# Attention and two MLPs on one core: h banks and scratch blocks as tensors of their own, the cosine of a pair in two halves, other figures in the build-time planner

## The chip, the cores and the metric

The kernel runs on one core of a Trainium2 chip. The metric is device time in microseconds (us), the median of several runs. Three runs of the kernel before took 893.64, 894.47 and 897.54 us; 894.47 us is the time before.

## The reference, cut to what matters

```python
def reference(q, k, v, w_in, w_out, s, b, w2_in, w2_out):
    x = attention(q, k, v)          # 4 x 8 heads, 576 positions, head size 64; heads 0-3: window of 32,
                                    # heads 4-7: 32 positions at a distance of 4; softmax
    x = x.transpose(0, 2, 1, 3).reshape(2304, 512)
    h = x @ w_in                    # 512 -> 2048
    x = (s * np.maximum(h, 0) ** 2 + b) @ w_out     # 2048 -> 512
    h = x @ w2_in                   # 512 -> 2048
    return (h * np.cos(h)) @ w2_out # 2048 -> 512
```

All of it is fp32. The kernel splits an fp32 operand into a high part in fp32r and the rest, and makes one product of three fp32r matmuls.

## The kernel before, in words

**First part, attention and the first MLP** (line 1060 on). The 2304 tokens go in five tiles of 384, 384, 512, 512 and 512 (`SIZES`). Within a tile the loop runs over 16 chunks of the hidden size: `mm_in` makes h in a PSUM bank, `relu2` squares it, `mm_out` accumulates y in four banks. Attention for the next tile, the unpacking of the weights from 64-bit words (`w_float`, `w_join`) and the preparation of the second MLP's weights (`pair_*`) are laid beside these matmuls. `y_out(t)` (line 651) evicts the four y banks of a tile, two on ACT and two on DVE, and writes the tile to the DRAM tensor `parked`: on SP's queue in one DMA for tiles 0 to 3, and for tile 4 in four DMAs on ACT's queue, one behind each eviction.

**Second part, the second MLP** (`second_mlp`, line 728). The tokens go in three stretches of 768 (s = 0, 1, 2), each in two halves of 384 columns (`TH`). Both matrix products are done by Strassen and Winograd's scheme with seven products where a plain 2 x 2 division has eight. For a pair j of hidden chunks the seven products i = 1, 5, 6, 3, 7, 2, 4 are six matmuls of 384 columns each: such a group of six is called a step below. `h_mm` (line 841) loads the step's weights `w_in` on SP's queue (eight buffers in turn), makes the matmuls into a bank, and evicts it: i = 1, 5, 6 by a copy on ACT (`hp`, `hu`), i = 4 by a copy on ACT into `hh`, i = 3, 7, 2 by an add on DVE into `hh`. Products 6, 7 and 4 of a pair go on accumulating in the bank of product 1, and 3 in that of 5. The order on TensorE is 1(j), 2(j-1), 5(j), 6(j), 4(j-1), 3(j), 7(j), then 1(j+1), where (j) says the pair. The banks are: `j % 2` for 1, 6, 7, 4; number 2 for 5 and 3; number 3 for 2. The eight PSUM banks are four tiles of two banks each, `bank[0..3]`; h has the last two:

```python
        bank = [psum.tile([P, 2, 512], F32, tag=f"b{n}", name=f"bank{n}") for n in range(4)]
            b = j % 2 if i in (1, 6, 7, 4) else 2 if i in (5, 3) else 3
            acc = bank[2 + b // 2][:, b % 2, :TH]
```

So bank 0 of h lies beside bank 1 in one tile, and bank 2 beside bank 3. After 4(j) comes `cosine(s, j)` (line 864): ACT takes h + 0.25 to whole turns, DVE subtracts, ACT takes the sine, and DVE multiplies by h in two halves into `group`. `turns` is one buffer. The second product (`y_mm`, line 795) reads `group` through `ring` (split on ACT and DVE) and the weights `w_out`. The first 58 h steps of stretch 0 run alone; from there h steps of stretch 1 and y steps of stretch 0 alternate, and so on, until y steps of stretch 2 run alone. `x_steps(s)` (line 761) loads the four quarters of a stretch from `parked` into a `group` buffer and makes the seven left operands of it (`xo`) with subtractions and splits on ACT and DVE. For stretch 0 this is done during the first part (`first_x`, lines 1087 to 1101).

**What sets the order.** The program is scheduled by hand: every engine and queue executes its instructions in the order in which they are given out. That order comes from the planner `Recorder` (lines 83 to 273), which runs when the kernel is built. It records the instructions, keeps the order of TensorE's, and gives each of the others a due time from what needs it. `length` (line 187) says how long each instruction occupies its engine and how much later its result is there; `HOP` is added where one engine waits for another. `order` then goes through time: whenever an engine is free it takes, of the instructions whose needs are met within `LOOK` (0.4 us), the one due first. `give_out` issues a batch; a batch is given out whole before the next one is recorded. Tile 4's `y_out` belongs to the batch of line 1102, and the whole second part (its first `w_in` load too) to the next, line 1108. Waits between engines are not the planner's: the framework adds them from the tiles that the instructions, in the order given, write and read. All instructions of planned batches carry line 272 in the profile, so that rows are told apart by tile names.

Of the kernel before, what the change touches and what calls it, by code (L numbers as in the profile page):

```python
# [9 lines left out]
F32 = mybir.dt.float32  # L10
# [4 lines left out]
AF = mybir.ActivationFunctionType  # L15
ALU = mybir.AluOpType
# [5 lines left out]
NT = B * S  # L22
P = 128
# [59 lines left out]
class Recorder:  # L83
# [1 line left out]

    HOP, LOOK, SOON, EARLIER = 0.12, 0.4, 4.0, 4.0
    ENGINES = {"tensor": "PE", "vector": "DVE", "scalar": "ACT", "sync": "SP", "gpsimd": "POOL"}

    def __init__(self, nc):
# [94 lines left out]
    @staticmethod  # L186
    def length(engine, what, out, args, kw, aps):
        cols = math.prod(k for _, k in out.ap[1:])
        if what == "dma_start":
            moved = cols * out.ap[0][1] * mybir.dt.size(out.dtype) / 280.0e3  # L190
            return (0.06, 2.6 + 1.5 * moved) if engine == "scalar" else (moved, 2.6 + 0.5 * moved)
        if engine == "tensor":
            if what == "transpose":
                return 0.00085 * cols, 0.0
            if args[1].dtype == F32R:
                return cols / 2400.0 + 0.0133, 0.0
            return (4 * cols / 2400.0 + 0.0053) * (0.6 if cols <= 64 else 1.0 if cols > 300 else 1.25), 0.0
        if engine == "scalar":
            extra = 0.09 if is_pointer(kw) else 0.0
            return 0.19 + 0.000833 * cols + extra + (0.19 if kw.get("accum_out") is not None else 0.0), 0.0  # L200
        from_psum = any(x.space == bass.MemoryType.PSUM for x in aps)
        if what == "tensor_reduce":
            cols = math.prod(k for _, k in kw["in_"].ap[1:])
            return 0.15 + 0.00107 * cols, 0.0
        two = what in ("tensor_tensor", "scalar_tensor_tensor") or from_psum
        return 0.152 + (0.001047 if two else 0.00054) * cols, 0.0

    def order(self):

        steps, ids = self.steps, self.kept  # L210
        own = set(ids)
        hop = lambda a, b: self.HOP if steps[a][0] != steps[b][0] else 0.0
        due = {}
        for n in reversed(ids):
            if steps[n][0] == "PE" or steps[n][5] or n not in due:
                due[n] = min(due.get(n, 1.0e9), steps[n][4])
            for d in steps[n][3] & own:
                due[d] = min(due.get(d, 1.0e9), due[n] - hop(d, n) - steps[d][1] - steps[d][2])
        left, then, ready = {}, {n: [] for n in ids}, {}
        for n in ids:  # L220
            left[n] = len(steps[n][3] & own)
            ready[n] = max((self.ends[d] + hop(d, n) for d in steps[n][3] - own), default=-1.0e9)
            for d in steps[n][3] & own:
                then[d].append(n)
        pe = [n for n in reversed(ids) if steps[n][0] == "PE"]
        waiting, free = {e: [] for e in self.free}, dict(self.free)
        for n in ids:
            if not left[n] and steps[n][0] != "PE":
                waiting[steps[n][0]].append(n)
        given = []  # L230
        while len(given) < len(ids):
            best = None
            for e, able in waiting.items():
                if e == "PE":
                    able = [n for n in pe[-1:] if not left[n]]
                if not able:
                    continue
                first = max(free[e], min(ready[n] for n in able)) + (0.0 if e == "PE" else self.LOOK)
                n = min((n for n in able if ready[n] <= first), key=lambda n: (due[n], n))
                at = max(free[e], ready[n])  # L240
                if best is None or (at, n) < best[:2]:
                    best = (at, n, e)
            at, n, e = best
            given.append((at, n))
            free[e] = at + steps[n][1]
            self.ends[n] = free[e] + steps[n][2]
            if e == "PE":
                pe.pop()
            else:
                waiting[e].remove(n)  # L250
            for k in then[n]:
                ready[k] = max(ready[k], self.ends[n] + hop(n, k))
# [28 lines left out]
def attention_then_two_mlps(ctx, tc, qk_p, qk_d, v_p, v_d, mask_p, mask_d, w1, w2, sv, bv, out):  # L281
# [39 lines left out]
        nc.scalar.copy(xy_tile(t)[:, :, :n], spill[:, :, :n])  # L321

    scratch = pool("scratch", 1, ctx, space=bass.MemoryType.DRAM)
    parked = scratch.tile([P, NCC, NT], F32, tag="parked", name="parked")
    cut_in = [scratch.tile([P, 7, 2, 256], F32, tag=f"cut_in{j}", name=f"cut_in{j}") for j in range(NPAIR)]
    cut_out = scratch.tile([P, 7, NPAIR, 2, 256], F32, tag="cut_out", name="cut_out")

# [321 lines left out]
            nc.tensor.matmul(y[:, : SIZES[t]], lo, g[:, 0, :], start=False, stop=fc == NFC - 1)  # L649

    def y_out(t):
        to = parked[:, :, STARTS[t] : STARTS[t + 1]]
        for e in range(NCC):
            y = yps[t][e]
            if t == 0:
                nc.vector.tensor_scalar_mul(bsum[:, e : e + 1], y[:, SIZES[0] : SIZES[0] + 1], b_sb)
            dst, bias = xy[t][:, e, :], bsum[:, e : e + 1]
            if e % 2 == 0:
                nc.scalar.activation(out=dst, in_=y[:, : SIZES[t]], func=AF.Identity, scale=s_sb, bias=bias)
            else:  # L660
                nc.vector.tensor_scalar(
                    out=dst, in0=y[:, : SIZES[t]], scalar1=s_sb, scalar2=bias, op0=ALU.mult, op1=ALU.add
                )
            if t == NTILE - 1:
                nc.scalar.dma_start(to[:, e, :], dst)
        if t < NTILE - 1:
            nc.sync.dma_start(to, xy[t])
        del xy[t], yps[t]

    def g_tile(t, fc):  # L670
# [33 lines left out]
    def x_loads(s, places):  # L704
        def load(place, key):
            rows, half = BLOCKS[key]
            t0 = s * TS + half * TH
            nc.sync.dma_start(place, parked[:, 2 * rows : 2 * rows + 2, t0 : t0 + TH])

        return [lambda p=p, key=key: load(p, key) for p, key in zip(places, X_BLOCKS)]  # L710

# [16 lines left out]
    def second_mlp(pool, psum, first_x):  # L728
# [8 lines left out]
        yp1, yp5, yu2, yc21 = (pool.tile([P, 2, TH], F32, tag=x, name=x) for x in ("yp1", "yp5", "yu2", "yc21"))  # L737
        for n in range(6, N_X):
            x_slot[n] = pool.tile([P, 2, 2, TH], F32R, tag=f"xo{n}", name=f"xo{n}")
        bank = [psum.tile([P, 2, 512], F32, tag=f"b{n}", name=f"bank{n}") for n in range(4)]  # L740

        places = {
            0: dict(X=(0, 2), Y=(1, 3)),
# [51 lines left out]
        def y_mm(s, i, j):  # L795
            r, w = splits[s, i, j // 2]
            b, new = Y_BANK[s == NS - 1][i]
            for half in range(2):
                cs = slice(half * P, (half + 1) * P)
                for k, (a, x) in enumerate(((0, 0), (0, 1), (1, 0))):  # L800
                    nc.tensor.matmul(
                        bank[b][:, half, :TH], w[:, j % 2, a, cs], r[:, x, j % 2, :],
                        start=new and j == 0 and k == 0, stop=j == NPAIR - 1 and k == 2, skip_group_check=True,
                    )

        def y_end(s, i):
            last = s == NS - 1
            acc = lambda i: bank[Y_BANK[last][i][0]][:, :, :TH]

            def send(tile, row, half):  # L810
                t0 = s * TS + half * TH
# [5 lines left out]
                nc.scalar.copy(yp5, acc(5))  # L817
            elif i == 6:
                nc.scalar.copy(yu2, acc(6))
                plus(yu2, acc(3), yu2)  # L820
                if last:
                    plus(yu2, yp5, yu2)
                send(yu2, 256, 1)
            elif i == 2:
                plus(yp1, acc(2), yp1)
                send(yp1, 256, 0)
            elif i == 7:
                if last:
# [12 lines left out]
        def h_mm(s, j, i):  # L841
# [1 line left out]
            loads[0] += 1  # L843
            nc.sync.dma_start(w.bitcast(F32), cut_in[j][:, IN_AT[i]])
            b = j % 2 if i in (1, 6, 7, 4) else 2 if i in (5, 3) else 3
            acc = bank[2 + b // 2][:, b % 2, :TH]
            x = x_slot[operand[s, i]]
            for kc in range(2):
                cs = slice(kc * P, (kc + 1) * P)
# [23 lines left out]

        x_makes(0, first_x)[-1]()
        h_list = []
# [7 lines left out]

        def h_step(s, j, i):
            h_mm(s, j, i)
            if i == 4:
                cosine(s, j)
                if j == NPAIR - 1:
                    whole[0] = s + 1
                    if s + 1 < NS:  # L890
                        x_steps(s + 1)
# [305 lines left out]
```

## Time and profile before

| | |
|---|---|
| median of 3 runs | 894.47 us (893.64 to 897.54) |
| the profiled execution | 895.13 us |
| its span, first to last instruction | 893.3 us |
| TensorE (PE) busy | 859.4 us, 96% |
| PE's weight loads (PEld) busy | 755.9 us, 85% |
| VectorE (DVE) busy | 646.6 us, 72% |
| ScalarE (ACT) busy | 529.7 us, 59% |
| mean granted clock of TensorE | 0.991 |

Times in rows are microseconds from the start of the span. A matmul's row starts when it is taken up; matmuls overlap, so the busy time of one (0.34 us) is about twice the distance to the next. The granted clock is a share of 2.4 GHz. "x12" is the number of instructions that a row merges, and a bracket at its end the idle time before it and what ended that. SPq and ACTq are the queues on which DMAs are issued. Buffer numbers are left out of names: `hp` stands for `hp10`, `hp11` and `hp5`, `hu` for `hu2`, `bank` for all four.

### The profile page before, as it was taken

What the parts mean: (1) busy time and instruction counts of PE and PEld (TensorE: products, weight loads), DVE (VectorE), ACT (ScalarE), POOL (GpSimd) and SP (SyncE); (2) the same over time, 40 slices, a digit from 0 to 9 for tenths busy, and PEclk for the clock granted to TensorE, in tenths of its full rate; (3) what the DMA queues carried; (4) which work ended last, traced back from release to release, by engine and by line L of the source; (5) the groups of instructions that cost most, each with busy time, mean ns of one, the idle gap of its engine ahead of it and who ended that gap; (6) DMA issues with size and microseconds to landing.
All of it is one profiled execution on the core that took longest, in us unless ns stands there. A gap on an engine that the chain in (4) does not pass through costs nothing.

```text
span 893.3 us, 13668 instructions
## 1 busy us (share of the span) xinstructions
PE 859.4 (96%) x5004; PEld 755.9 (85%) x5004; DVE 646.6 (72%) x1062; ACT 529.7 (59%) x1060; POOL 3.5 (0%) x10
## 2 busy tenths in 40 slices
PE   8999999999999999999999678899999999999998
PEld 6656689998888888888888577699999999999997
DVE  6899899767655676668778335588777878767783
ACT  6888885666556555556555235576555655655642
POOL 1000000000000000000000000000000000000000
PEclk9999999999999999999999979999999999999999
DMA  9977425456426256653876666668788888896786
GB/s 253 345 252 237 131 92 165 145 172 225 134 100 220 76 197 204 202 188 124 264 263 199 210 214 196 203 205 256 229 265 269 290 268 249 276 277 204 228 261 212
DMA packets 97826, 189.85 MB, mean 213 GB/s; under 512 B 8320, under 2 KB 48736, under 8 KB 97760
## 3 DMA queue, kind: packets, MB, share of 16 engines
q1 hardware_dynamic: 97184, 187.94, 66.3%
q10 hardware_dynamic: 576, 1.05, 0.3%
q8 instruction: 40, 0.66, 0.3%
q14 instruction: 26, 0.21, 0.1%
HBM read 150.16 MB, written 38.80 MB: 212 GB/s over the span
## 4 chain that ended last, share of the span: by engine, by line
PE 90%; DMA 4%; DVE 3%; ACT 2%; issue 0%; SPq 0%; DVEq 0%; ACTq 0%
PE bank L272 40%; PE y L272 22%; PE h L272 22%; PE sc L272 3%; PE pv L272 2%; PE tp L272 1%; DVE hh L272 1%; DMA first_v<-v_d 1%; DMA stage<-w 1%; DVE wa L272 1%; DMA group<-parked 1%; DMA first_v<-v_p 1%; DMA first_qk<-qk_d 0%; DMA first_qk<-qk_p 0%; ACT wa L272 0%
## 5 line engine op out<-in xcount | busy, mean ns | idle before, releaser
L272 PE MATMUL bank<-xo,w_in 128*128 128x384 f32 x1008 | 202.9, 342 | 24.6 <-DVE hh L272 19.5
L272 PEld LDWEIGHTS bank<-xo,w_in 128*128 128x128 f32 x1008 | 177.7, 190 | 34.7 <-DVE hh L272 25.9
L272 PE MATMUL bank<-ring,w_out 128*128 128x384 f32 x1008 | 193.4, 336 | 0.9 <-ACT yc L272 0.9
L272 PEld LDWEIGHTS bank<-ring,w_out 128*128 128x128 f32 x1008 | 176.6, 188 | 2.8 <-ACT yc L272 1.4
L272 PE MATMUL h<-xs,wh 128*128 128x512 f32 (+1 forms) x512 | 153.5, 381 | 0.0
L272 PE MATMUL y<-g,wh 128*128 128x512 f32 (+1 forms) x512 | 152.3, 379 | 0.0
L272 ACT CAST ring<-group 128x768 fp32r<-128x768 f32 x84 | 69.8, 834 | 67.5 <-PE bank L272 66.7
L272 PEld LDWEIGHTS h<-xs,wh 128*128 128x128 f32 x512 | 93.7, 188 | 15.0
L272 PEld LDWEIGHTS y<-g,wh 128*128 128x128 f32 x512 | 94.1, 188 | 14.4
L272 ACT ACTIVATE r<-h 128x512 f32<-128x512 f32 (+1 forms) x80 | 44.2, 553 | 102.5 <-PE h L272 100.1
L272 DVE TENSOR_TENSOR ring<-group,ring 128x768 fp32r<-128x768 f32 x84 | 79.7, 955 | 23.9 <-ACT ring L272 22.8
L272 PE MATMUL h<-xs,wl 128*128 128x512 f32 (+1 forms) x256 | 96.4, 376 | 0.0
L272 PE MATMUL y<-g,wl 128*128 128x512 f32 (+1 forms) x256 | 96.2, 376 | 0.0
L272 ACT ACTIVATE sm<-sm,nmax 96x80 f32<-96x80 f32 (+1 forms) x140 | 49.4, 354 | 13.6 <-DVE nmax L272 13.6
L272 PEld LDWEIGHTS h<-xs,wl 128*128 128x128 f32 x256 | 48.1, 188 | 7.6
L272 PEld LDWEIGHTS y<-g,wl 128*128 128x128 f32 x256 | 48.0, 188 | 7.6
L272 ACT COPY hp<-bank 128x384 f32<-128x384 f32 x48 | 23.0, 480 | 50.8 <-PE bank L272 45.4
L272 DVE CAST g<-r 128x512 fp32r<-128x512 f32 (+1 forms) x64 | 25.9, 405 | 35.5 <-ACT r L272 35.4
L272 DVE TENSOR_TENSOR group<-turns,hh 128x768 f32<-128x768 f32 x48 | 44.1, 953 | 7.9 <-ACT turns L272 7.9
L272 DVE SCALAR_TENSOR_TENSOR turns<-turns,hh 128x1536 f32<-128x1536 int32 x24 | 42.0, 1751 | 7.8 <-ACT turns L272 7.8
L272 PE MATMUL y<-g,wa 128*128 128x385 f32 x128 | 44.2, 488 | 0.0
L272 PE MATMUL h<-xy,wa 128*128 128x384 f32 x128 | 44.0, 490 | 0.0
(109 smaller groups left out, 1111.7 us busy)
## 6 DMA issues: line engine op xcount, KB each, us to landing
w_in<-cut_in SPq DMA_DIRECT2D x168, 256.0 KB, 3.6
w_out<-cut_out SPq DMA_DIRECT2D x84, 512.0 KB, 4.3
stage<-w SPq DMA_DIRECT2D x32, 512.0 KB, 5.2
raw<-w SPq DMA_DIRECT2D x32, 512.0 KB, 5.8
cut_in<-w SPq DMA_DIRECT2D x8, 896.0 KB, 5.4
cut_out<-w SPq DMA_DIRECT2D x8, 896.0 KB, 5.3
qk<-qk_d SPq DMA_DIRECT2D x20, 352.0 KB, 4.3
qk<-qk_p SPq DMA_DIRECT2D x20, 304.0 KB, 3.4
```

Source lines behind the costliest of these rows:

```text
L272: getattr(getattr(self.nc, engine), what)(*args, **kw)
```

## The change

- `parked` becomes six tensors of 384 columns. `y_out` writes a tile in as many DMAs as it meets blocks (tiles 2, 3 and 4: two each), all on SP's queue after the whole tile's evictions; tile 4's four DMAs on ACT's queue go. `x_loads` reads from the block that it needs.
- h has four PSUM tiles of one bank each; y keeps two of two banks. In the last stretch y's products 3 and 2 use h banks; they are evicted by two adds of 384 columns in place of one of 768.
- The cosine is made in halves of 768 columns: the second half of `hh` after step 7 (its chunks come from 3 and 7), the first half after step 4.
- In the planner, `HOP` was 0.12 us for all. It is now 0.21 us behind PE, 2.0 us behind an SP DMA that ACT or DVE waits for, and 0.05 us for all else, an SP DMA that PE waits for among it. 0.09 us of each ACT and DVE instruction's length are counted as delay of its result and no longer as time of its engine.

```diff
-    HOP, LOOK, SOON, EARLIER = 0.12, 0.4, 4.0, 4.0
+    LOOK, SOON, EARLIER = 0.4, 4.0, 4.0
+    HOP = {"PE": 0.21, "SP": 2.0}
...
-            return 0.19 + 0.000833 * cols + extra + (0.19 if kw.get("accum_out") is not None else 0.0), 0.0
+            return 0.10 + 0.000833 * cols + extra, 0.09
...
-        return 0.152 + (0.001047 if two else 0.00054) * cols, 0.0
+        return 0.062 + (0.001047 if two else 0.00054) * cols, 0.09
...
-        hop = lambda a, b: self.HOP if steps[a][0] != steps[b][0] else 0.0
+        hop = lambda a, b: 0.0 if steps[a][0] == steps[b][0] else self.HOP.get(
+            steps[a][0] if steps[b][0] != "PE" or steps[a][0] != "SP" else "", 0.05
+        )
...
-    parked = scratch.tile([P, NCC, NT], F32, tag="parked", name="parked")
+    parked = [scratch.tile([P, NCC, TH], F32, tag=f"parked{b}", name=f"parked{b}") for b in range(NT // TH)]
...
-            if t == NTILE - 1:
-                nc.scalar.dma_start(to[:, e, :], dst)
-        if t < NTILE - 1:
-            nc.sync.dma_start(to, xy[t])
+        for b in range(NT // TH):
+            lo, hi = max(STARTS[t], b * TH), min(STARTS[t + 1], (b + 1) * TH)
+            if lo < hi:
+                nc.sync.dma_start(
+                    parked[b][:, :, lo - b * TH : hi - b * TH], xy[t][:, :, lo - STARTS[t] : hi - STARTS[t]]
+                )
...
-            nc.sync.dma_start(place, parked[:, 2 * rows : 2 * rows + 2, t0 : t0 + TH])
+            nc.sync.dma_start(place, parked[2 * s + half][:, 2 * rows : 2 * rows + 2, :])
...
-        bank = [psum.tile([P, 2, 512], F32, tag=f"b{n}", name=f"bank{n}") for n in range(4)]
+        y_bank = [psum.tile([P, 2, 512], F32, tag=f"by{n}", name=f"y_bank{n}") for n in range(2)]
+        h_bank = [psum.tile([P, 512], F32, tag=f"bh{n}", name=f"h_bank{n}") for n in range(4)]
...
-            acc = bank[2 + b // 2][:, b % 2, :TH]
+            acc = h_bank[b][:, :TH]
...
-        def cosine(s, j):
-            h, rest = hh[(s * NPAIR + j) % 2], turns.bitcast(F32)
-            nc.scalar.activation(out=turns, in_=h, func=AF.Identity, bias=quarter)
-            nc.vector.scalar_tensor_tensor(out=rest, in0=turns, scalar=-1.0, in1=h, op0=ALU.mult, op1=ALU.add)
+        def cosine(s, j, n):
+            half = slice(2 * n, 2 * n + 2)
+            h, turn = hh[(s * NPAIR + j) % 2][:, half, :], turns[:, half, :]
+            rest = turn.bitcast(F32)
+            nc.scalar.activation(out=turn, in_=h, func=AF.Identity, bias=quarter)
+            nc.vector.scalar_tensor_tensor(out=rest, in0=turn, scalar=-1.0, in1=h, op0=ALU.mult, op1=ALU.add)
             nc.scalar.activation(out=rest, in_=rest, func=AF.Sin, scale=TWO_PI, bias=right_angle)
-            for n, key in enumerate(("11", "12")):
-                g, _, k = g_place(s, key, j)
-                half = slice(2 * n, 2 * n + 2)
-                nc.vector.tensor_tensor(out=g[:, :, k, :], in0=rest[:, half, :], in1=h[:, half, :], op=ALU.mult)
+            g, _, k = g_place(s, ("11", "12")[n], j)
+            nc.vector.tensor_tensor(out=g[:, :, k, :], in0=rest, in1=h, op=ALU.mult)
...
-            if i == 4:
-                cosine(s, j)
+            if i in (7, 4):
+                cosine(s, j, int(i == 7))
```

## Rows read from the trace of the kernel before

**Rows 1.** Stages: length; PE, PEld, DVE, ACT, POOL busy; granted clock; DMA.
```profile
25.00:125.00 100.00, 98.71 (x480) 63.18 (x478) 92.48 (x186) 85.69 (x201) 0.00 (x0) 1.00 0.66 217
125.00:500.00 375.00, 375.00 (x2299) 324.60 (x2299) 264.30 (x515) 219.40 (x538) 0.00 (x0) 1.00 0.53 174
...
509.30:523.00 13.70, 7.24 (x21) 6.44 (x21) 5.05 (x7) 1.21 (x3) 0.00 (x0) 0.50 0.85 309
523.00:592.60 69.60, 57.84 (x300) 51.11 (x300) 41.37 (x48) 39.63 (x50) 0.00 (x0) 1.00 0.67 191
...
592.60:893.30 300.70, 292.04 (x1664) 287.99 (x1662) 225.84 (x256) 165.03 (x200) 0.00 (x0) 1.00 0.81 252
```

**Rows 2.** PE's waits, 500 to 592.6: total us, times, longest.
```profile
PE bank L272 <- DVE hh L272: 16.3, 13, 8.5
PE bank L272 <- ACT hu L272: 2.9, 5, 0.6
PE bank L272 <- ACT hh L272: 1.7, 3, 0.6
```

**Rows 3.** Timeline, 561 to 566: start, us, what, idle before.
```profile
561.69 0.48 ACT L272 COPY hu<-bank 128x384 f32<-128x384 f32 x1 [0.75 <-PE bank L272]
...
562.22 2.35 PE L272 MATMUL bank<-xo,w_in 128*128 128x384 f32 x12 [0.57 <-ACT hu L272]
...
564.61 0.48 ACT L272 COPY hh<-bank 128x384 f32<-128x384 f32 x1 [0.96 <-PE bank L272]
...
565.14 2.39 PE L272 MATMUL bank<-xo,w_in 128*128 128x384 f32 x12 [0.57 <-ACT hh L272]
```

**Rows 4.** Timeline of PE where the second part begins.
```profile
499.89 4.41 PE L272 MATMUL bank<-xo,w_in 128*128 128x384 f32 x24
504.65 1.99 PE L272 MATMUL bank<-xo,w_in 128*128 128x384 f32 x10 [0.35 <-DMA w_in<-cut_in]
515.11 3.25 PE L272 MATMUL bank<-xo,w_in 128*128 128x384 f32 x9 [8.47 <-DVE hh L272]
```

**Rows 5.** Timeline of DVE in the same stretch.
```profile
500.10 0.81 DVE L272 TENSOR_SCALAR xy<-y,s_sb,bsum 128x512 f32<-128x512 f32 x1 [0.55 <-PE y L272]
511.43 0.96 DVE L272 TENSOR_TENSOR group<-group 128x768 f32<-128x768 f32 x1 [10.53 <-DMA group<-parked]
...
514.51 0.55 DVE L272 TENSOR_TENSOR hh<-bank,hp 128x384 f32<-128x384 f32 x1
```

**Rows 6.** Timeline of SP's queue in the same stretch.
```profile
478.79 25.81 SPq L272 DMA_DIRECT2D w_in<-cut_in  x8
504.69 1.41 SPq L272 DMA_DIRECT2D group<-parked  x3
```

**Rows 7.** Waits of SP's queue, 478 to 506.
```profile
SPq L272 <- DMA parked<-xy: 18.9, 4, 16.6
```

**Rows 8.** Groups by shape, 500.0 to 592.6: busy us, mean ns, idle before.
```profile
L272 DVE SCALAR_TENSOR_TENSOR turns<-turns,hh 128x1536 f32<-128x1536 int32 x7 | 12.3, 1751 | 0.7 <-ACT turns L272 0.7
L272 ACT ACTIVATE turns<-hh,quarter 128x1536 int32<-128x1536 f32 x7 | 11.1, 1580 | 3.1 <-DVE group L272 3.0
L272 DVE TENSOR_TENSOR group<-turns,hh 128x768 f32<-128x768 f32 x12 | 11.0, 955 | 5.4 <-ACT turns L272 5.4
...
L272 ACT CAST xo<-group 128x768 fp32r<-128x768 f32 x6 | 5.0, 834 | 5.0 <-DMA group<-parked 5.0
...
L272 ACT COPY hu<-bank 128x384 f32<-128x384 f32 x8 | 3.8, 476 | 5.1 <-PE bank L272 5.0
```

**Rows 9.** DMAs, 490:600 and 318:327: count, KB, us to landing.
```profile
w_in<-cut_in SPq DMA_DIRECT2D x66, 256.0 KB, 3.1
...
parked<-xy SPq DMA_DIRECT2D x1, 1024.0 KB, 4.4
```

**Rows 10.** Chain that ended last: the y steps that run alone.
```profile
830.36 58.56 PE bank L272 x336
```

**Rows 11.** Waits of PE, 592.6 to the end.
```profile
PE bank L272 <- DVE hh L272: 3.3, 5, 0.7
```

More of the change, by code (lines that the diff above doesn't have):

```diff
@@ L198, in length @@
         if engine == "scalar":
-            extra = 0.09 if is_pointer(kw) else 0.0
-            return 0.19 + 0.000833 * cols + extra + (0.19 if kw.get("accum_out") is not None else 0.0), 0.0
+            extra = (0.09 if is_pointer(kw) else 0.0) + (0.19 if kw.get("accum_out") is not None else 0.0)
+            return 0.10 + 0.000833 * cols + extra, 0.09
         from_psum = any(x.space == bass.MemoryType.PSUM for x in aps)
@@ L203, in length @@
             cols = math.prod(k for _, k in kw["in_"].ap[1:])
-            return 0.15 + 0.00107 * cols, 0.0
+            return 0.06 + 0.00107 * cols, 0.09
         two = what in ("tensor_tensor", "scalar_tensor_tensor") or from_psum
-        return 0.152 + (0.001047 if two else 0.00054) * cols, 0.0
+        return 0.062 + (0.001047 if two else 0.00054) * cols, 0.09
     def order(self):
@@ L651, in y_out @@
     def y_out(t):
-        to = parked[:, :, STARTS[t] : STARTS[t + 1]]
         for e in range(NCC):
@@ L706, in load @@
             rows, half = BLOCKS[key]
-            t0 = s * TS + half * TH
-            nc.sync.dma_start(place, parked[:, 2 * rows : 2 * rows + 2, t0 : t0 + TH])
+            nc.sync.dma_start(place, parked[2 * s + half][:, 2 * rows : 2 * rows + 2, :])
         return [lambda p=p, key=key: load(p, key) for p, key in zip(places, X_BLOCKS)]
@@ L739, in second_mlp, with y_half @@
             x_slot[n] = pool.tile([P, 2, 2, TH], F32R, tag=f"xo{n}", name=f"xo{n}")
-        bank = [psum.tile([P, 2, 512], F32, tag=f"b{n}", name=f"bank{n}") for n in range(4)]
+        y_bank = [psum.tile([P, 2, 512], F32, tag=f"by{n}", name=f"y_bank{n}") for n in range(2)]
+        h_bank = [psum.tile([P, 512], F32, tag=f"bh{n}", name=f"h_bank{n}") for n in range(4)]
+        def y_half(b, half):
+            return y_bank[b][:, half, :TH] if b < 2 else h_bank[2 * (b - 2) + half][:, :TH]
         places = {
@@ L801, in y_mm @@
                     nc.tensor.matmul(
-                        bank[b][:, half, :TH], w[:, j % 2, a, cs], r[:, x, j % 2, :],
+                        y_half(b, half), w[:, j % 2, a, cs], r[:, x, j % 2, :],
                         start=new and j == 0 and k == 0, stop=j == NPAIR - 1 and k == 2, skip_group_check=True,
@@ L807, in y_end, with add @@
             last = s == NS - 1
-            acc = lambda i: bank[Y_BANK[last][i][0]][:, :, :TH]
+            acc = lambda i: y_bank[Y_BANK[last][i][0]][:, :, :TH]
+            def add(tile, i):
+                b = Y_BANK[last][i][0]
+                if b < 2:
+                    plus(tile, acc(i), tile)
+                else:
+                    for half in range(2):
+                        plus(tile[:, half, :], y_half(b, half), tile[:, half, :])
             def send(tile, row, half):
@@ L819, in y_end @@
                 nc.scalar.copy(yu2, acc(6))
-                plus(yu2, acc(3), yu2)
+                add(yu2, 3)
                 if last:
@@ L824, in y_end @@
             elif i == 2:
-                plus(yp1, acc(2), yp1)
+                add(yp1, 2)
                 send(yp1, 256, 0)
@@ L885, in h_step @@
             h_mm(s, j, i)
-            if i == 4:
-                cosine(s, j)
-                if j == NPAIR - 1:
+            if i in (7, 4):
+                cosine(s, j, int(i == 7))
+                if (i, j) == (4, NPAIR - 1):
                     whole[0] = s + 1
```

## The prediction

> **What bounds the kernel now.** Read the busy time by stage first [rows 1]. TensorE (PE, the first engine column) is busy in 375.00 of the 375.00 us from 125 to 500 and in 292.04 of the last 300.70, so neither stretch can give much. It stands still from 500 to 592.6, in the first stretch of the second MLP, where h steps run alone. No other engine is full there: from 523 on DVE is busy in 41.37 of 69.60 us and ACT in 39.63. The reader is to see a stage without a saturated engine, hence one made of waits.
>
> The waits of PE name them [rows 2]: 21, of which one is 8.5 us and the other 20 together 12.4 (7.8 on DVE's `hh`, 2.9 and 1.7 on ACT's copies).
>
> Take the twenty first, in the timeline [rows 3]. PE waits for the ACT copy `hu`, which evicts step 6. The step that follows in the written order is 4 of the pair before, in the neighbouring bank. It runs, and 3 after it: 12 matmuls, two steps. Then PE waits for the copy into `hh`, which evicts that 4, although the next step is 7, back in 6's bank. No step needs data of the one that it waits for. What the two share is the tile: banks 0 and 1 of h are one tensor, so are 2 and 3. The other waits of the list fit this: 7 before 1 and 2 before 5, both added by DVE, are neighbours too. That the waits come from the tensor and not from the order is a reading of four rows and the code; the rival for it is below.
>
> The 8.5 us stop is read from three timelines. PE makes 24 and 10 matmuls and then stands until 515.11 [rows 4]. DVE's `hh` add ending at 515.06 releases it; that add stood in DVE's queue behind a subtraction on `group`, which waited for the `group` loads until 511.43 [rows 5]. These loads were issued at 504.69, behind eight `w_in` loads spread over 25.81 us [rows 6], and SP spent 16.6 us of that in one wait for the writes of `parked` on ACT's queue [rows 7]. After the stop the granted clock is 0.50, 1.2 GHz, from 509.3 to 523.0 [rows 1]; before and after it is 2.4 GHz.
>
> **The change part by part.** The price of a matmul at full clock comes from the 336 of the end: 58.56 / 336 = 0.1743 us [rows 10]. The first 58 h steps are 348 matmuls, 60.7 us; at present they last from 499.89 to 592.6, 92.7 us.
>
> *h banks of their own.* The 20 waits go. From 515.11 to 592.6 PE makes the other 348 - 34 = 314 matmuls [rows 4], 54.7 us, and 3.7 more because 21 of them run at half clock [rows 1]; 77.5 - 58.4 = 19.1 us are left for 20 stops, 0.95 each (0.62 of it shown as a gap, the rest the overlap that a stop breaks). The true waits that stay have two steps, 2.1 us, between the eviction's cause and its reader (1 to 6, 5 to 3, 6 to 7). A copy takes 0.476 us [rows 8], so an engine may come 1.5 us late. That is enough when it is held by one 768-column instruction (0.834 to 0.955), and tight behind one of 1536 (1.58 to 1.75). I leave 2 us of residual stops: the bounds are 0 and 9.5, half of today's.
>
> *The cosine in halves.* Per pair, ACT: four of 0.834 in place of two of 1.580, 0.18 us more, 24 pairs, 4.2 us. DVE: two of 0.955 in place of one of 1.751, 0.16 more, 3.8 us in all [rows 8]. At full pace a pair lasts 7.3 us, in which ACT has 4 x 0.48 + 4 x 0.83 = 5.3 and DVE about 5.5 us of evictions and cosine. Both fit, so the splitting costs nothing, its cover being those 2 us per pair; if the cover fails, it costs at most the 4.2 us.
> The Trainium skill speaks against small instructions ("VectorE: DVE Perf Modes", the section on the TRN2 errata for SBUF sources): its table gives each ScalarE instruction 224 cycles of fixed cost, 0.19 us at 1.2 GHz, and advises large tiles. By that the 48 further ACT instructions would cost 9.0 us of ACT and the sum, with ACT below PE still, would not move; the rows give 0.088 each.
>
> *`parked` by blocks, on SP.* The four ACT issues go, and with them the 16.6 us wait. But in the order given out, tile 4's two writes now stand on SP ahead of every `w_in` load, since their batch comes first, and they wait for the last eviction, which ends at 500.91 [rows 5]. Two issues of about 0.47 (1.41 / 3 [rows 6]) bring the first `w_in` to about 501.9. Ahead of it in the queue is 1 MB of writes; such a write takes 4.4 us from issue [rows 9], to 505.4, and 256 KB more, at the 309 GB/s of 509.3 to 523 [rows 1], 0.8. So the h steps begin at 506.2 in place of 499.9 [rows 4], a new stop of 6.3 us where there was none. Bounds: 505.0, a usual 3.1 us load [rows 9] not delayed by the writes; 508, if the 512-byte pieces of the 128-column block halve the speed. The stop halves the clock as today's does: it came back 7.9 us after PE resumed at 515.11 [rows 1, 4], so I charge 7.9 / 2 = 4.0 us (bounds 0 and 6).
> The Trainium skill ("DMA: Bandwidth & Descriptors", "Issuing engines are not separate DMA queues") says that the issuing engine matters only for the time of the issue. By it the move from ACT to SP would be free; it leaves out that SP's later issues wait with the write, and is weighed as a rival.
>
> *What follows in SP's queue.* Today the `group` loads of stretch 1 follow the eighth `w_in` at once [rows 6]: no ninth could be asked for before the first step ended and gave its buffer back, and SP had time. Now SP comes late, and when it has issued eight `w_in` the ninth is already due first. The `group` loads are due some 50 us later. So the subtraction on `group` leaves the head of DVE's queue and the 8.5 us stop goes with it. Who is late next: the loads, sums and splits for stretch 1 crowd into the last 10 us before it. Four sums of 0.955 are added there; from 0 to 4 us, I take 2.
>
> *Stretch 1 on.* Five waits of the same kind [rows 11] go: 5 x 0.95 = 4.8 us (none to all). The two split adds of the last stretch (4 x 0.55 [rows 5] for 2 x 0.96, 0.3 us of DVE) lie beside matmuls.
>
> *The planner's figures in the first part.* Four more DMA issues on SP and another order there. PE is full, so it can't gain but for 1.3 us of idle in 25 to 125; DVE, at 92.48 of 100 us [rows 1], can lose. From -1.3 to +4 I take +0.5.
>
> Sum, in the profiled execution of 895.13 us: the 92.7 us become 6.3 + 60.7 + 4.0 + 2.0 = 73.0, 19.7 less; then 2.0 more for crowding, 4.8 less, 0.5 more: 22.0 less, 873.1. The median of the runs stands 0.66 below that execution: **872.5 us**.
>
> **The rivals.**
>
> *Two true waits for one false.* The order is static, and if ACT and DVE are planned close to their limit, half of the 20 stops come back as real ones: 9.5 for the 2.0, and 4 for crowding in place of 2: 882 us. For it: ACT and DVE each have over 70% of a pair's 7.3 us, and splits for `ring` and `xo` besides. Against: two steps of slack and instructions of half the length. 0.16.
>
> *The start is free.* If the first loads don't wait for the writes, the 6.3 us stop and the half clock go, 10.3 us: 862. For it, the Trainium skill's sentence above. Against: the first four loads were issued at 478.79 and on only because no waiting write stood before them on SP. 0.08 for it or for something near it (a short stop, the clock kept).
>
> *The tensors are not the cause.* Then the split of the banks does nothing, 19.1 + 4.8 us stay, at that pace without residual stops or crowding, and only the transition changes: 872.5 + 23.9 - 4 = 892. Against: neighbours in all three kinds of wait. 0.06.
>
> *Slower: the weights come late.* From 25 to 125 us PE uses weights as DVE unpacks them, in 32 chunks, with 7.5 us of DVE idle in the stage [rows 1]. If the planner, counting 2.0 us behind each SP DMA, sets a chunk's float and join behind other work and DVE idles meanwhile, PE waits. At 2 us for each chunk it loses 32 x 2 - 7.5 = 56 us, and the time would be 929; it decides against the change from 1.05 us a chunk, where the loss (26 us) passes the gain of 22 by 0.5%. Against: the delay is added for all chunks alike, so that it shifts them once and doesn't stretch their distance, and the stage loads run five ahead. 0.04.
>
> **How the numbers follow.** The forecast has 0.66, with its own range from 866 to 880 by the bounds of its terms, which won't all fall on one side. The range to hold 8 in 10 reaches up past the first rival and down to the second's edge: 863 to 884. A measurement of this kernel tells some 0.5%, 4.5 us, from no change. Faster than 890: the forecast, the first and second rival, 0.90; the third lies within the bound, with a part of the fourth, 0.06; slower 0.04.
>
> **What would show it.** Right: in the waits of PE for the first stretch, `hh` and `hu` almost gone; a run of many steps without a break; a PE stop from 500 to about 506, ended by `w_in`, with SP's writes of `parked` issued just before; granted clock 0.50 for some 8 us after; `group` loads issued near 550 and not at 504; the h steps alone ending near 573. Wrong: stops of 0.6 us still at neighbouring banks; a DVE or ACT wait of several us with evictions queued behind it; PE under 98 us in 25 to 125.

## The result, and the profile after

The changed kernel takes **872.39 us**, the median of four runs (871.16 to 872.85); the kernel before, on the same chip, took 894.70 (four runs, 893.64 to 897.54). The ratio is 0.9744, with a 95% interval of 0.9719 to 0.9768: 2.6% faster. The forecast was 872.5 in a range of 863 to 884. In the changed kernel planned instructions carry line 275.

The profiled execution took 872.85 us, 22.28 less than that of before. By stage, with the first and the last instruction of each read from TensorE's timeline:

| stage | before | after | difference |
|---|---|---|---|
| first part, to the end of its last y matmul | 500.06 | 502.84 | +2.78 |
| from there to the first y matmul of the second part | 92.61 | 71.82 | -20.79 |
| from there to the end of the span | 300.63 | 296.44 | -4.19 |
| around the span | 1.83 | 1.75 | -0.08 |

Stages of the kernel after, columns as in [rows 1]:

```profile
25.00:125.00 100.00, 98.03 (x469) 62.30 (x468) 93.96 (x184) 87.03 (x193) 0.00 (x0) 0.98 0.65 216
125.00:500.00 375.00, 374.94 (x2298) 324.07 (x2297) 260.57 (x516) 217.20 (x542) 0.00 (x0) 1.00 0.53 172
506.90:513.70 6.80, 3.54 (x11) 3.57 (x12) 0.00 (x0) 0.48 (x1) 0.00 (x0) 0.50 1.03 346
513.70:574.60 60.90, 60.31 (x345) 59.62 (x344) 46.10 (x62) 45.75 (x70) 0.00 (x0) 1.00 0.86 277
```

Once it runs, the h stage is full: PE is busy in 60.31 of 60.90 us, with ACT and DVE at three quarters. PE's waits from 495 to 580 (us in total, times, longest):

```profile
PE h_bank L275 <- DMA w_in<-cut_in: 7.9, 2, 7.3
```

This one line stands where [rows 2] has three: no wait on an eviction is left. PE's timeline, first in the first part, then at the start of the second:

```profile
35.81 4.54 PE L275 MATMUL y<-g,wa 128*128 128x385 f32 x8 [1.97 <-ACT g L275]
...
502.45 0.39 PE L275 MATMUL y<-g,wl 128*128 128x512 f32 x1
510.16 20.08 PE L275 MATMUL h_bank<-xo,w_in 128*128 128x384 f32 x104 [7.33 <-DMA w_in<-cut_in]
```

SP's issues around the start, and where the `group` loads went:

```profile
503.76 1.21 SPq L275 DMA_DIRECT2D parked<-xy  x2
...
558.40 1.37 SPq L275 DMA_DIRECT2D group<-parked  x3
559.87 2.31 SPq L275 DMA_DIRECT2D w_in<-cut_in  x3
```

And the part of the chain of waits from the first `w_in` on:

```profile
505.06 4.97 DMA w_in<-cut_in
510.16 49.71 PE h_bank L275 x275
559.87 6.92 DMA w_in<-cut_in
566.93 5.67 PE h_bank L275 x30
```

SP issues the last tile's writes at 503.76 and the first `w_in` load behind them at 505.06; it lands 4.97 us later, and PE has stood still for 7.33 us. From 510.16 on PE runs 312 matmuls without a break (the chain follows 275 of them, up to the issue at 559.87). The next `w_in` load that matters is issued at 559.87, behind three `group` loads, needs 6.92 us, and costs 0.59.

### The profile page after: what moved, and what is told of

The parts are those of the page before. It is cut to its first block, busy times and chain, and to the rows that moved or that the text cites. A ratio compares the mean times of both kernels' runs of the same rounds, so it can differ in the third digit from the quotient of the medians.

```text
span 871.1 us, 13713 instructions
## 1 busy us (share of the span) xinstructions
PE 851.4 (98%) x5004; PEld 755.9 (87%) x5004; DVE 646.3 (74%) x1088; ACT 539.2 (62%) x1108; POOL 3.5 (0%) x10
## 4 chain that ended last, share of the span: by engine, by line
PE 91%; DMA 4%; DVE 2%; ACT 1%; SPq 1%; issue 0%; ACTq 0%; DVEq 0%
PE y L275 23%; PE h L275 22%; PE h_bank L275 21%; PE y_bank L275 18%; PE sc L275 3%; PE pv L275 2%; DMA stage<-w 2%; PE tp L275 2%; DMA w_in<-cut_in 1%; DVE w L275 1%; DMA first_v<-v_d 1%; DMA first_qk<-qk_d 1%; DVE group L275 0%; SPq L475 0%; SPq L474 0%
## 5 line engine op out<-in xcount | busy, mean ns | idle before, releaser
L275 PE MATMUL h_bank<-xo,w_in 128*128 128x384 f32 x1008 | 194.1, 337 | 8.6 <-DMA w_in<-cut_in 7.9
L275 PEld LDWEIGHTS h_bank<-xo,w_in 128*128 128x128 f32 x1008 | 177.6, 189 | 10.1 <-issue 7.7
L275 PE MATMUL y_bank<-ring,w_out 128*128 128x384 f32 x912 | 176.8, 336 | 0.9 <-ACT yc L275 0.9
L275 PEld LDWEIGHTS y_bank<-ring,w_out 128*128 128x128 f32 x912 | 160.1, 188 | 2.5 <-ACT yc L275 1.5
L275 DVE SCALAR_TENSOR_TENSOR turns<-turns,hh 128x768 f32<-128x768 int32 x48 | 45.7, 954 | 19.3 <-ACT turns L275 18.4
L275 ACT ACTIVATE turns<-turns,right_angle 128x768 f32<-128x768 f32 x48 | 44.7, 938 | 23.2 <-DVE turns L275 23.0
L275 DVE TENSOR_TENSOR group<-turns,hh 128x768 f32<-128x768 f32 x48 | 45.7, 955 | 12.5 <-ACT turns L275 11.9
L275 ACT ACTIVATE turns<-hh,quarter 128x768 int32<-128x768 f32 x48 | 45.1, 939 | 9.9 <-DVE hh L275 8.9
L275 PE MATMUL y<-g,wa 128*128 128x385 f32 x128 | 46.0, 504 | 2.0 <-ACT g L275 2.0
```

The costliest lines, as they stand in the source:

```text
L275: getattr(getattr(self.nc, engine), what)(*args, **kw)
```

## The experiments

Times are medians of four runs or more, ratios those to the kernel before run beside them.

### 1. The banks alone, both ways

**The kernel after with its h banks two by two in a tensor again:**

```diff
-        h_bank = [psum.tile([P, 512], F32, tag=f"bh{n}", name=f"h_bank{n}") for n in range(4)]
+        h_two = [psum.tile([P, 2, 512], F32, tag=f"bh{n}", name=f"h_bank{n}") for n in range(2)]
+        h_bank = [h_two[n // 2][:, n % 2, :] for n in range(4)]
```

> The changed kernel with the four h banks put back two by two into one tensor; all else as changed. Theory (the short stops come from the shared tensor): the stops of about 0.6 us on evictions in the neighbouring bank come back, some 20 while h steps run alone and some 5 after, at 0.95 us each: 24 us on the changed kernel's 872.4, 896 us; the stop at the start of the second part stays at about 7 us. Rival (the stops came from the static order and the load of ACT and DVE, which the halves and the planner's figures changed): the split of the banks does nothing, 872 us, and PE's waits on hh and hu stay near zero.

900.53 us, ratio 1.0064 (1.0043 to 1.0086). PE's waits of this kernel from 500 to 592:

```profile
PE h_bank L275 <- DVE hh L275: 9.1, 14, 0.7
PE h_bank L275 <- DMA w_in<-cut_in: 7.3, 1, 7.3
PE h_bank L275 <- ACT hu L275: 4.0, 7, 0.6
PE h_bank L275 <- ACT hh L275: 0.8, 2, 0.6
```

The short stops of [rows 2]'s kind are back, 23 of them where the kernel before had 20, the stop on `w_in` is as it was, and the kernel is 28.1 us slower than the one after: without the split all the rest of the change is a loss of 0.6%. That is 4.5 us more than expected. Behind the h stage there are ten such stops on `hh` (5.6 us in all, the longest 1.48) and not five, and the time from the first y matmul of the second part on is 9.7 us longer than in the kernel after.

**The kernel before with nothing but the split of the banks** (y's last products use h banks there as in the change):

```diff
-        bank = [psum.tile([P, 2, 512], F32, tag=f"b{n}", name=f"bank{n}") for n in range(4)]
+        y_bank = [psum.tile([P, 2, 512], F32, tag=f"by{n}", name=f"y_bank{n}") for n in range(2)]
+        h_bank = [psum.tile([P, 512], F32, tag=f"bh{n}", name=f"h_bank{n}") for n in range(4)]
...
-            acc = bank[2 + b // 2][:, b % 2, :TH]
+            acc = h_bank[b][:, :TH]
```

> The kernel before with the h banks split into four tensors, and nothing else of the change (whole cosine, one parked tensor, the four writes on ACT's queue, old planner figures). Theory: the 20 short stops and the five later ones go (24 us), the stop of 8.5 us where the second part begins stays or grows to the landing of the ninth w_in load at 516.9: 894.7 - 24 = 871 us, if the whole cosine's 1.6 to 1.75 us instructions bring no true waits; with half of the stops back as true waits, 880. Rival (the stops come from order and load): 895 us.

871.35 us, ratio 0.9732 (0.9707 to 0.9757). PE's timeline:

```profile
499.99 4.40 PE L272 MATMUL h_bank<-xo,w_in 128*128 128x384 f32 x24
505.04 3.42 PE L272 MATMUL h_bank<-xo,w_in 128*128 128x384 f32 x18 [0.64 <-DMA w_in<-cut_in]
514.51 2.29 PE L272 MATMUL h_bank<-xo,w_in 128*128 128x384 f32 x6 [6.05 <-DVE hh L272]
517.78 12.46 PE L272 MATMUL h_bank<-xo,w_in 128*128 128x384 f32 x54 [0.99 <-DMA w_in<-cut_in]
```

The short stops are gone, the long one of before [rows 4] stays, at 6.05 us. This is the whole gain: 871.35 against 872.39. The other three edits together move nothing that the measurement can tell (1.0 us, within the spread of the runs).

### 2. The cosine and the planner's figures

**The kernel after with the whole cosine of before:**

```diff
-            if i in (7, 4):
-                cosine(s, j, int(i == 7))
+            if i == 4:
+                cosine(s, j)
```

> The changed kernel with the cosine of a pair made whole again after step 4; all else as changed. Theory (two steps of slack leave an engine 1.5 us, an instruction of 1.6 to 1.75 us breaks that now and then): PE's waits on hh, hp and hu come back for some of the eight pairs of stretch 0, 2 to 10 us in all, 875 to 882 us. Rival (the slack suffices anyway, as the planner puts the long instructions between the copies): 872 us, with 24 x 0.3 us less busy time on ACT and DVE and no gain from it.

876.65 us, ratio 0.9792 (0.9763 to 0.982): the halves are worth 4.3 us in the kernel after. The time is in the range expected, but not for the reason: of the waits on evictions in stretch 0 only one of 0.64 us, on `hp`, came back. 2.8 us lie at the start of stretch 1, where the `group` loads now come late; the rest is not located. DVE's and PE's timeline there:

```profile
581.73 1.75 DVE L275 SCALAR_TENSOR_TENSOR turns<-turns,hh 128x1536 f32<-128x1536 int32 x1
583.39 0.95 DVE L275 TENSOR_TENSOR xo<-group,xo 128x768 fp32r<-128x768 f32 x1
...
584.40 1.19 PE L275 MATMUL h_bank<-xo,w_in 128*128 128x384 f32 x5 [1.72 <-DVE xo L275]
```

and the stretch behind it, columns as in [rows 1]:

```profile
585.40:588.80 3.40, 3.40 (x12) 3.40 (x11) 3.37 (x4) 2.37 (x3) 0.00 (x0) 0.51 0.39 150
```

An operand of stretch 1 stands on DVE behind a 1536-column instruction of 1.75 us, PE waits 1.72, and the granted clock is 0.51 for 3.4 us after it, some 1.7 lost. With the halves the same wait on `xo` is 0.66 and the clock stays:

```profile
583.04 1.15 PE L275 MATMUL h_bank<-xo,w_in 128*128 128x384 f32 x5 [0.66 <-DVE xo L275]
```

In the kernel with the split of the banks alone, where the `group` loads come early, the cosine is whole too and no stop on `xo` shows.

**The kernel after with the planner's old figures** (the lines of the diff in `length` and `hop`, taken back):

```diff
-    HOP = {"PE": 0.21, "SP": 2.0}
+    HOP, LOOK, SOON, EARLIER = 0.12, 0.4, 4.0, 4.0
...
-            return 0.10 + 0.000833 * cols + extra, 0.09
+            return 0.19 + 0.000833 * cols + extra + (0.19 if kw.get("accum_out") is not None else 0.0), 0.0
```

> The changed kernel with the planner's old figures (0.12 us behind any engine, no delay counted apart); all else as changed. Theory of the prediction (the figures cost in the first part and do little in the second): the 2.0 us stop of PE near 36 us goes, the first part ends some 2.8 us earlier, at 499.7, and the second part is as changed or up to 3 us longer: 869 to 873 us. Rival (the new figures are what keeps ACT and DVE in step with PE in the second part): true waits while h steps run alone, and group operations ahead of evictions in DVE's queue again, 5 us or more: 877 us and over.

870.98 us, ratio 0.973 (0.9704 to 0.9756). In its trace the first part ends at 499.63 in place of 502.84, and the stop on `w_in` is 7.33 us as in the kernel after: the new figures cost the first part some 3 us in these two executions, and they are not what makes the stop. Over all kernels here the first part ends at 499.6 to 500.2 with the old figures and at 501.7 to 503.7 with the new ones. The stop near 36 us, which was expected to go, is still 1.49 us with the old figures, without half clock behind it.

### 3. The stop at the start: the last tile's writes on another queue

```diff
-                nc.sync.dma_start(
+                (nc.scalar if t == NTILE - 1 else nc.sync).dma_start(
```

The second kernel has `nc.gpsimd` there.

> The changed kernel with the last tile's two block writes on ACT's queue in place of SP's; all else as changed. Theory (SP's own in-order queue made the 7.3 us stop: two writes waiting for the last eviction stand ahead of all w_in loads): the stop of 7.3 us and the half clock behind it (6.8 us at half, some 1.8 lost) go or shrink to 2 us, as in the kernel before loads may wait for ACT's writes from the seventh on; 872.4 - 7 = 865 us (863 to 868). Rival (the first loads would be late anyway, behind the writes in the DMA engines whichever queue issues them): 871 to 873.

> The changed kernel with the last tile's two block writes on GpSimd's queue, which has nothing else to do then; all else as changed. Theory: no load on SP waits for the writes in any way, the h steps follow the first part without a stop and without half clock, and the group loads of stretch 1 come early again, so that the crowding before stretch 1 goes as well: 872.4 - 7.3 - 1.8 - 1 = 862 us. Rival (the loads are late whichever queue issues the writes): 871 to 873.

On ACT 870.99 us, ratio 0.9726 (0.9711 to 0.9741); on GpSimd 873.12, ratio 0.9752 (0.9737 to 0.9767). Neither gained the 7 to 10 us. With the writes on ACT, PE's, SP's, ACT's and DVE's timeline:

```profile
512.64 5.99 PE L275 MATMUL h_bank<-xo,w_in 128*128 128x384 f32 x24 [5.79 <-ACT hu L275]
...
482.22 25.74 SPq L275 DMA_DIRECT2D w_in<-cut_in  x8
508.06 1.33 SPq L275 DMA_DIRECT2D group<-parked  x3
...
511.38 0.83 ACT L275 CAST xo<-group 128x768 fp32r<-128x768 f32 x1 [5.89 <-DMA group<-parked]
...
515.61 0.96 DVE L275 TENSOR_TENSOR group<-group 128x768 f32<-128x768 f32 x1 [9.51 <-DMA group<-parked]
```

The stop on `w_in` went, and that of before came back in its place: the planner put the `group` loads behind the eighth `w_in` again, and ACT's and DVE's work on `group` stood ahead of evictions. With the writes on GpSimd, PE's and SP's timeline:

```profile
519.19 11.08 PE L275 MATMUL h_bank<-xo,w_in 128*128 128x384 f32 x49 [7.48 <-DMA w_in<-cut_in]
...
501.69 1.27 SPq L275 DMA_DIRECT2D group<-parked  x3
512.32 0.80 SPq L275 DMA_DIRECT2D w_out<-cut_out  x2
513.16 0.43 SPq L275 DMA_DIRECT2D group<-parked  x1
513.69 5.08 SPq L275 DMA_DIRECT2D w_in<-cut_in  x8
```

and SP's waits from 495 to 515:

```profile
SPq L275 <- PE y L275: 13.6, 1, 13.6
SPq L275 <- DMA parked<-xy: 9.2, 1, 9.2
```

Here the `group` and `w_out` loads stand ahead of the ninth `w_in`; the first wait for the last y matmul, the second for the writes on GpSimd, and the ninth `w_in`, which could have gone near 503, when the first step (from 501.72) was done with its buffer, is issued at 513.69.

The same two with the planner's old figures:

> The changed kernel with the planner's old figures and the last tile's two block writes on ACT's queue. If the two effects add (old figures 2.2 us in the first part, writes 7): 863 us. If the old figures put the group subtraction ahead of evictions in DVE's queue again, as in the kernel before, a stop of some 6 to 8 us comes back near 510: 870 us.

> The changed kernel with the planner's old figures and the last tile's two block writes on GpSimd's queue. If the effects add: 862 - 2 = 860 us. With the group loads early and landed long before DVE comes to the subtraction, the order of DVE's queue has no price: no stop near 510 with either set of figures. Otherwise 866 us and over.

871.28 us, ratio 0.9732 (0.9717 to 0.9747), with a stop of 7.03 on `hh` at 515.32; and 871.65, ratio 0.9736 (0.9719 to 0.9752), with one of 8.54 on `w_in` at 518.61. So the stop needs more than the writes: whichever queue has them, SP has something in front of a `w_in` load that can't go before the first part is over, or the work on `group` blocks the evictions.

### 4. The writes moved, and SP's order kept

If that is so, the writes have to leave SP's queue *and* the `w_in` loads have to stay ahead of the loads for stretch 1. The planner is told that SP is late, as it is in the kernel after, so that SP's order there stays but for the writes:

```diff
+        rec.free["SP"] = max(rec.free["SP"], rec.free["PE"] - 6.5)
         second_mlp(later, banks, first_x)
```

with the writes on GpSimd, then the same with the old figures, then with the writes on ACT:

> The kernel after with the last tile's two writes of parked issued on GpSimd, and with the planner told that SP comes free 6.5 us later than it thinks at the start of the second part, so that the order on SP stays that of the kernel after: eight and more w_in loads in front, w_out and group loads some 50 us later. Theory (the stop at the start of the second part is SP's queue standing still behind something that needs the end of the first part: tile 4's writes in the kernel after, the w_out and group loads in the runs with the writes moved): now nothing of the kind stands ahead of a w_in load, so no stop of several us between 500 and 525, no half clock there, h steps alone done near 565, time 862 to 865. Rival (w_in loads are late because the DMA engines are full with the writes, whoever issues them): a stop of 3 us or more on w_in between 503 and 525 stays, time 869 or more.

> The same two edits with the planner's figures of before. Theory: as in the kernel with the new figures but for the first part, which was 2 to 3 us shorter with the old ones: 860 to 863. If the old figures place the w_out loads ahead of a ninth w_in again, the stop stays and the time is 869 to 872.

> The kernel after with the last tile's two writes on ACT's queue and the same 6.5 us for SP in the planner. In the earlier run with the writes on ACT, SP stood 17.5 us in one wait for these writes ahead of its last early w_in loads, and then came the group loads. Theory: that wait stays (it is not the order that makes it), the group loads go to the end of the stage: a stop of 1 to 2 us on w_in at most and no stop on hu or hh, 864 to 867. Rival (the wait itself makes the loads late): a stop of 5 us or more on w_in between 510 and 525, 870 or more.

863.38 us, ratio 0.965 (0.9621 to 0.9679); **860.91 us, ratio 0.9619 (0.9592 to 0.9646)**, the fastest kernel of this study, 11.5 us below the kernel after; and 864.59, ratio 0.9659 (0.9627 to 0.9691). The fastest one's stages, columns as in [rows 1]:

```profile
125.00:500.00 375.00, 375.00 (x2300) 324.59 (x2299) 264.11 (x515) 219.49 (x537) 0.00 (x0) 1.00 0.54 177
500.00:562.90 62.90, 62.24 (x355) 61.32 (x354) 47.89 (x64) 46.95 (x73) 1.56 (x2) 1.00 0.86 285
```

and its chain of waits through the start of the second part:

```profile
491.81 8.16 PE y L272 x36
499.97 55.38 PE h_bank L272 x318
```

PE goes from y to h without a gap, the clock is 1.00 throughout, and the h stage lasts 62.9 us, where 354 matmuls at 0.1743 make 61.7. Between the kernels of 873.12 and 863.38 only the line on SP's order differs, so it, and not the DMA engines' load, decides. That line without the move of the writes was not run.

In the third kernel, PE's timeline:

```profile
506.51 5.55 PE L275 MATMUL h_bank<-xo,w_in 128*128 128x384 f32 x30 [0.65 <-ACT hp L275]
512.63 2.61 PE L275 MATMUL h_bank<-xo,w_in 128*128 128x384 f32 x13 [0.58 <-DVE turns L275]
```

and SP's waits from 485 to 515:

```profile
SPq L275 <- DMA parked<-xy: 19.6, 2, 17.6
```

SP's wait of 17.6 us for the writes on ACT's queue is still there, between the sixth and the seventh `w_in`; a second one of 2.0 us precedes the eighth. PE hardly feels them: six steps of weights are in place, and no load for stretch 1 follows. The stop of 0.58 us that ends at 512.63 stands with DVE in the profile, but the eighth `w_in`, issued at 509.73, lands at 512.50, and its step is the one that PE waits to begin. The 0.65 before it is ACT's: it issues the two writes from 504.67 to 505.93 and copies `hp` only then. Together they are as much as the 1.2 us between this kernel and that of 863.38. What the 16.6 us wait of before [rows 7] cost there, where loads for stretch 1 do follow, this does not show.

### 5. Which figure costs the first part

The kernel of 863.38 with the old instruction lengths and the new `HOP`:

```diff
-            return 0.10 + 0.000833 * cols + extra, 0.09
+            return 0.19 + 0.000833 * cols + extra, 0.0
...
-        return 0.062 + (0.001047 if two else 0.00054) * cols, 0.09
+        return 0.152 + (0.001047 if two else 0.00054) * cols, 0.0
```

> The kernel with the writes on GpSimd and SP 6.5 us later (new figures, 863.38), with the old instruction lengths (no 0.09 us of them counted as delay) but the new HOP. In the order that results, ACT makes the relu of the first h before the third conversion of the weights, as with all the old figures; with the new lengths it stands behind that conversion. Theory (the 2 to 3 us lost in the first part are the stop at 36 us, and that is this one place in ACT's order, with a later load behind it; the lengths put it there): the stop at 34 to 36 us shrinks from 2.9 us to under 1, no half clock there, the first part ends near 500, the time is 860 to 861.5. Rival (the 2.0 us counted behind SP's loads makes the loss): the stop at 36 us and the end of the first part at 503 stay, 863 to 864.

865.42 us, ratio 0.9662 (0.9631 to 0.9692): missed. The stop at 36 us did go, but others took its place. PE's and DVE's timeline:

```profile
372.11 0.77 PE L275 MATMUL tp<-ident,sm 96*80 96x96 f32 x4 [2.15 <-DVE sm L275]
...
505.23 4.93 PE L275 MATMUL h_bank<-xo,w_in 128*128 128x384 f32 x27
...
368.88 1.29 DVE L275 CUSTOM_DVE_ANT_0 w<-raw,w 128x1024 uint16<-128x1024 uint16 x2
370.20 0.43 DVE L275 TENSOR_TENSOR w<-w 128x256 f32<-128x256 f32 x1
370.55 0.16 DVE L275 TENSOR_SCALAR ssum<-ssum 96x4 f32<-96x4 f32 x1
```

A softmax stands on DVE among preparations of weights, PE waits 2.15 us, and the first part ends at 505.39. The lengths explain a part of the stop at 36 us: in the new order ACT's relu of the first h stands behind one more conversion of weights, 0.6 us. The rest varies with the landing of the weights that ACT converts before it: ACT takes them up at 31.61 in the kernel after, at 29.75 in that of before and at 29.91 here, and with all the old figures the stop was between nothing and 1.49 us. That the lengths are the whole of the loss is not shown: with either set of lengths the new `HOP` gave a first part that ends later than with the old figures together.

## Why the prediction was right

- **The h banks.** Right in cause, place and size. The forecast took 19.1 us from the h stage and 4.8 from later; split alone, the banks gave 23.0, and paired again in the kernel after they cost 28.1, 19.1 of it in the h stage (90.9 against 71.8). One count was off: 59 steps, 354 matmuls, stand before the first y matmul and not 58; that is 1.05 us on both sides, so a stop cost 0.90 and not 0.95.
- **Residual true waits, 2.0.** None is left in the stage; the rival of two true waits for one is out.
- **The start.** Right in mechanism and order: writes on SP, then `w_in`, then PE. The stop was 7.33 us for 6.3, from the end of y at 502.84 to PE's start at 510.16, behind the landing of `w_in`; with the old figures, the first part ending at 499.63, it was 7.33 as well, so it is the time of the DMAs that was taken 1 us short: 4.97 us for the load where the forecast had 4.3, and 0.4 more for the two issues in front of it.
- **Half clock, 4.0.** Too much. The granted clock was 0.50 until 513.7, 3.54 us after PE resumed, so 1.8 us. In before it came back 7.9 us after, and in the kernel with the split alone (resumed at 514.51, with one more stop of 0.99) 9.4 us after. The step that failed is to take one such time for all.
- With these the stage adds up: 7.33 + 61.7 + 1.8 + 0.59 = 71.4 of the 71.82 measured.
- **`group` loads late, crowding, 2.0.** Right: issued at 558.40, and the two stops that follow are 0.59 and 0.66.
- **Later stops, 4.8.** The last stage fell by 4.19, the 0.66 included.
- **Cosine in halves, at no cost.** It hid, as said, though it was larger than said. The page's groups of the kernel after:

```profile
L275 DVE SCALAR_TENSOR_TENSOR turns<-turns,hh 128x768 f32<-128x768 int32 x48 | 45.7, 954 | 19.3 <-ACT turns L275 18.4
L275 ACT ACTIVATE turns<-turns,right_angle 128x768 f32<-128x768 f32 x48 | 44.7, 938 | 23.2 <-DVE turns L275 23.0
L275 ACT ACTIVATE turns<-hh,quarter 128x768 int32<-128x768 f32 x48 | 45.1, 939 | 9.9 <-DVE hh L275 8.9
```

  DVE's 45.7 us are 3.7 more than 24 of 1.751 [rows 8], as forecast. ACT's 89.8 us are 14.0 more than 48 of 1.580, 0.29 for each further instruction, in place of 4.2: the halves take 0.938 and 0.939, not the 0.834 of the casts that stood for them. The Trainium skill ("VectorE: DVE Perf Modes", TRN2 errata for SBUF sources) has 224 cycles at 1.2 GHz, an estimated 0.19 us of fixed cost, nearer to the 0.29 than the 0.088 taken from the casts. By each of the three the sum is the same, since ACT is busy in 62% of the span. What the prediction missed is that the halves gain where the loads come late (4.3 us).
- **First part, +0.5.** The term that was most mis-sized: +2.78. It has a stop of 1.97 us on ACT's relu and 3.4 us of half clock behind it, at 36 us, in the engine (ACT) that the prediction did not look at there. The size is partly luck of the execution: in two more kernels with the same first part (h banks paired, whole cosine) it ended at 501.65 and 502.01, the stop was 1.62 and 1.36 us, and the clock stayed.
- **The sum** came out 0.25 us from the profiled execution because its errors cancel: 2.3 for the first part, 1.0 each for the longer stop and for the 59th step, and 0.4 unexplained, against 2.2 of half clock, 2.0 of residual waits and 0.8 of crowding.
- **The other rivals.** That the tensors are not the cause is refuted by both runs of the first pair. The weights don't come late chunk by chunk: PE is busy in 98.03 us of 25 to 125, if only just above the 98 set as a sign, and with 3.4 us of it at half clock behind the one stop at 36 us. The free start was a rival at 862 with 0.08, by the rule of the Trainium skill ("DMA: Bandwidth & Descriptors", Issuing engines are not separate DMA queues). Moving the writes alone between SP, ACT and GpSimd gave 872.39, 870.99 and 873.12, so by the totals the rule holds within 2.1 us, but only because the order behind the writes changed with them. With the order kept the same moves gave 863.38 and 864.59: against the rule, the queue of the writes is worth 7.8 to 9.0 us there, since SP's later loads wait behind them.

## What to carry to other kernels

Two accumulators that are used in turn should be tensors of their own, even if they would fit into one: the split of four PSUM banks was worth 23 of 894 us here, and the rest of the change together no gain that the measurement can tell. When a stop moves but doesn't shrink, look at what is queued in front of the late load, not only at what the load waits for: a queue in order needs everything ahead of its urgent entries to be ready as well. An edit that costs nothing in one order of the queues (the whole cosine) may cost 4 us in another, so undo parts one by one in the final kernel too.

## What was not expected of the hardware

- How long the clock stays at 1.2 GHz after PE resumes differed widely: 3.5 us in the kernel after, 7.9 in before, 9.4 with the split alone. In the two longer cases PE had run 34 and 42 matmuls of h, with one short stop, before it stood still; in the short one it had run none. That doesn't order the other runs: in the kernel of 870.99, with only the writes moved to ACT, PE had run 24, and the clock was back 3.4 us after it resumed. Before and the kernel with the split alone had one more stop (0.65 and 0.99) in the slow stretch; counted from the end of that stop, the times are 4.0 and 6.1 us. What decides is not settled by these runs.
- SP's `w_in` loads wait for writes of `parked` on ACT's queue, with which they share no data (17.5 and 17.6 us). The traces name what ties them. Each DMA has a semaphore (a counter) that tells of its landing, and the DMAs of SP and ACT take the same eight in turn. In the kernel of 864.59 the two writes have numbers 108 and 109, and so have the seventh and eighth `w_in`: the writes land at 507.33 and 509.71, and these loads are issued at 507.39 and 509.73. In the kernel before, four `w_in` follow the four writes in the same way, 0.02 to 0.07 us behind their landings. Writes on GpSimd have two others (111 and 112), and in the kernel of 863.38 no `w_in` waits for them.
- GpSimd issued its two writes 4.9 us apart (503.32 and 508.22), 4.05 of it idle with nothing that the profile shows to wait for. But the first write had landed at 507.90, and in all four kernels with these writes on GpSimd the second issue follows the first landing by 0.31 or 0.32 us. That it waits for that landing is likely, and not shown. The late second write is what the `w_out` loads waited for in the kernel of 873.12.
